# Maxima of a causal segment in whole rows of key blocks: fewer weight loads, diagonals copied from every bank

## The chip, the cores and the metric

The kernel runs on one core of a Trainium2 chip. The metric is the device time of one execution in microseconds; the median of several runs counts. TensorE is called PE (its weight loads PEld), VectorE DVE, ScalarE ACT, GpSimd POOL, and the queue that issues most DMAs SP.

## The reference

Two attention blocks with 32 heads of 16 dimensions read the same 2048 x 512 input, and a sigmoid gate mixes their outputs. Side A is full softmax attention over 2048 keys. Side B works in four segments of 512: causal softmax attention inside a segment, mixed with a linear memory of the earlier segments.

```python
def _B_ref(x, wq, wk, wv, wo, beta):
    ...
    ar = jnp.arange(L)
    mask = (ar[:, None] < ar[None, :]) * (-1e9)
    ...
    for s in range(N):
        qs, ks, vs = q[:, :, s], k[:, :, s], v[:, :, s]
        logits = jnp.einsum("bhqd,bhkd->bhqk", qs, ks) * scale + mask
        p = _softmax(logits, axis=-1)
        a_dot = jnp.einsum("bhqk,bhkd->bhqd", p, vs)
        ...
        o = g * a_mem + (1.0 - g) * a_dot
        ...

g = _sigmoid((x * gate_w).sum(-1, keepdims=True))
out = g * _A_ref(x, A_wqkv, A_wo) + (1 - g) * _B_ref(x, B_wq, B_wk, B_wv, B_wo, B_beta)
```

## The kernel before

The program has two parts. The first, about 330 us long, projects the input into queries, keys and values for both sides. The second, the main loop, does attention. Its work is cut into units: an A unit is four heads against one chunk of 512 queries and all 2048 keys; a B unit is four heads in one segment of 512 queries and keys. There are 32 of each, and in the main loop an A and a B unit alternate.

The order of all instructions is written out by hand in slots. An A unit has 64 slots, a B unit 10, so a pair has 74. A slot n has a score product into one of three PSUM banks `st` (line 652: 50 rows, 128 keys against 512 queries), an exponential on ACT (line 675, 672 for two of B's ten) and, 96 slots ahead for a later unit, one *part of maxima*: `max_part` (line 207) fills one of four PSUM banks `sm` by products (line 204), and the row maxima are taken from it. Maxima have to be known before the scores, because their negatives enter the score product as two extra rows. After every third slot comes a burst of value products (line 708) or of output products (line 785). Score products and products for maxima use different halves of the array's rows in turn, because heads 0, 1 lie in partitions 0 to 63 and heads 2, 3 in partitions 64 to 127; `r` says which half.

An A part is one product of 128 queries by 512 keys and one reduction by DVE (line 219) to one column. A B unit has ten parts, five for each half `r`, placed at every seventh slot of the 74, at slots 6, 13, 20, ... 69 (at every third slot for the first and for the last two units). In a segment of four blocks of 128, query block s needs key blocks 0 to s, the last of them under the causal mask. Before the change the five parts (i = 0 to 4) of a half are:

- i = 0, 1: four products of 128 columns, each a diagonal block of its own (query blocks 0 and 2, or 1 and 3, of two heads). ACT copies the bank to an SBUF tile `dg` (line 230), POOL masks it (`affine_select`, line 231), and eight slots later (`MASK_T`) DVE reduces the tile (line 234).
- i = 2, 3: query block 1 against key block 0 (128 columns) and query block 3 against key blocks 0 to 2 (384 columns), reduced by DVE from PSUM (line 240).
- i = 4: query block 2 against key blocks 0 and 1 for two heads (2 x 256 columns), reduced by DVE from PSUM (line 244).

So a bank was read either by ACT or by DVE. The tiles `dg` rotate through three buffers. The partial maxima lie in a tile `pmB`; nine slots after the unit's last part `finish_max` reduces them (line 182; line 180 for A), POOL rounds them, and eight slots and a little later PE transposes them (line 194). DVE's other work in the main loop is small: reciprocals and factors for the normalisation (lines 759 to 763).

Of the kernel before, what the change touches and what calls it, by code (L numbers as in the profile page):

```python
# [10 lines left out]
F32 = mybir.dt.float32  # L11
F32R = mybir.dt.float32r
AF = mybir.ActivationFunctionType
ALU = mybir.AluOpType
AX = mybir.AxisListType
# [7 lines left out]
CH = 512  # L23
# [24 lines left out]
def gated_mix(ctx, tc, x, xT, wqkv, a_wo, b_wq, b_wk, b_wv, b_wo, beta, gate_w, out):  # L48
    nc = tc.nc
# [43 lines left out]
    mp = ctx.enter_context(tc.tile_pool(name="mp", bufs=2))  # L93
# [18 lines left out]
    for k in range(NU):  # L112
        mine = {u: iter(range(32)) for u in range(2)}
        bs = [k - 1] if 0 < k < NU - 1 else [k - 1, k] if k else []
        start, apart = (34, 3) if k == 1 else (6, 7) if k < NU - 1 else (24, 3)
        theirs = {r: [(unit("B", b), (r, i)) for b in bs for i in range(5)] for r in range(2)}
        for p in range(64 + 10 * len(bs)):
            r = (len(maxs) + 1) % 2
            i = (p - start) // apart
# [42 lines left out]
    def rows(t, h, n):  # L162

        return t[64 * (h // 2):64 * (h // 2) + n, h % 2]
# [4 lines left out]
    late = []  # L169


    pmB = [mp.tile([128, 2, 4, 8], F32, name=f"pmB{i}", bufs=1) for i in range(2)]
    for t in pmB:
        nc.gpsimd.memset(t, -3.0e38)

    def finish_max(u):
        nm = mp.tile([128, 4, 4], F32, tag="nm", name="nm")
        pm = pmt.pop(u)
        if u[0] == "A":
            nc.vector.tensor_reduce(nm, pm, axis=AX.X, op=ALU.max, negate=True)  # L180
        else:
            nc.vector.tensor_reduce(nm.rearrange("p h (a b) -> p (h a) b", b=2),
                                    pm.rearrange("p b h (a k) -> p (h a) b k", a=2), axis=AX.X, op=ALU.max, negate=True)

        ms = mp.tile([128, 2, 2, 2, 4], F32R, tag="ms", name="ms")
        nv = nm.rearrange("p (r h) s -> p r h s", r=2)
        nc.gpsimd.tensor_copy(ms[:, :, 0], nv)  # L187
        nc.gpsimd.tensor_sub(ms[:, :, 1], nv, ms[:, :, 0].bitcast(F32))
        return ms
# [10 lines left out]
    def blocked(ps):  # L200
        return ps.rearrange("p (b t) -> p b t", t=128)

    def max_product(ps, u, h, s, n0, n, k, k0=0):
        nc.tensor.matmul(ps[:, n0:n0 + n], rows(qt[u][:, :, s * 128:(s + 1) * 128], h, 48), rows(k[:, :, k0:k0 + n], h, 48),  # L204
                         start=True, stop=True)

    def max_part(m, bank):

        u, (r, i) = maxs[m]
        side, g, c = u  # L210
        if u not in pmt:
            pmt[u] = mp.tile([128, 4, 4, 4], F32, tag="pmA", name="pm") if side == "A" else pmB[(c * NG + g) % 2]
        pm = pmt[u]
        ps = bank()
        if side == "A":

            kc, s, h = i // 8, i % 8 // 2, 2 * r + i % 2
            max_product(ps, u, h, s, 0, CH, kt_[u, kc])
            nc.vector.tensor_reduce(pm[:, h, s, kc:kc + 1], ps, axis=AX.X, op=ALU.max)  # L219
        else:  # L220


            k = kt_[u, c]
            h0 = 2 * r
            if i < 2:
                for n in range(4):
                    b = i + 2 * (n % 2)
                    max_product(ps, u, h0 + n // 2, b, 128 * n, 128, k, 128 * b)
                dg = dp.tile([128, 4, 128], F32, tag="dg", name="dg")
                nc.scalar.copy(dg, blocked(ps))  # L230
                nc.gpsimd.affine_select(out=dg, in_=dg, pattern=[[0, 4], [-1, 128]], base=0, channel_multiplier=1,  # L231
                                        compare_op=ALU.is_ge, fill=MASKED)
                to = pm[:, i, h0:h0 + 2, 3::4] if i == 0 else pm[:, i, h0:h0 + 2, 1::6]
                todo.append((m + MASK_T, lambda: nc.vector.tensor_reduce(  # L234
                    to, dg.rearrange("p (h s) t -> p h s t", h=2), axis=AX.X, op=ALU.max)))
            elif i < 4:
                h = h0 + i - 2
                max_product(ps, u, h, 1, 0, 128, k)
                max_product(ps, u, h, 3, 128, 384, k)
                nc.vector.tensor_reduce(pm[:, 1, h, 3:7], blocked(ps), axis=AX.X, op=ALU.max)  # L240
            else:
                for f in range(2):
                    max_product(ps, u, h0 + f, 2, 256 * f, 256, k)
                nc.vector.tensor_reduce(pm[:, 0, h0:h0 + 2, 4:6], ps.rearrange("p (h b t) -> p h b t", h=2, b=2), axis=AX.X,
                                        op=ALU.max)
        if m == last_max[u]:
            def finish():
                late.append((m + MASK_T + 2 + LATE_T, u, finish_max(u)))
            todo.append((m + (MASK_T + 1 if side == "B" else 0), finish))
# [28 lines left out]
    with ExitStack() as p0:  # L278
# [5 lines left out]
        wk1 = p0.enter_context(tc.tile_pool(name="wk1", bufs=1))  # L284
# [162 lines left out]
        def betas():  # L447

            ps = me_ps.tile([128, CH], F32, tag="me", name="bt")
            spread = wk1.tile([8, 2, 128], F32, name="spread")  # L450
            one8 = identf[0:8, 0:8]
            nc.vector.tensor_copy(spread[:, 0].rearrange("p (d h) -> p d h", h=8), one8.unsqueeze(1).broadcast_to([8, DH, 8]))
            nc.vector.tensor_copy(spread[:, 1].rearrange("p (h q) -> p h q", q=16), one8.unsqueeze(2).broadcast_to([8, 8, 16]))
            for i, to in enumerate((gh, ogh)):
                nc.tensor.matmul(ps[:, NO * i:NO * i + NO], spread[:, i], beta8, start=True, stop=True)
                nc.scalar.activation(to, ps[:, NO * i:NO * i + NO], AF.Sigmoid)
            nc.vector.tensor_scalar(ogh, ogh, -1.0, 1.0, op0=ALU.mult, op1=ALU.add)
        post_at(20, 2, betas)

        def gate_logit(xg, b, col):  # L460
# [82 lines left out]
        def some_max():  # L543
            m = mnext[0]
            if m == LEAD:
                return
            loads(m + 3 + PRE)
            for i in range(4):
                max_part(m + i, lambda: me_sm.tile([128, CH], F32, tag="sm", name="sm"))
            run_todo(m + 3)  # L550
            mnext[0] += 4
            run_late(me_ps, "me", mnext[0])
# [46 lines left out]
    dp = ctx.enter_context(tc.tile_pool(name="dp", bufs=3, reuse_waits="tile"))  # L599
# [257 lines left out]
    n = 0  # L857
    while n < nS or queue or beside or filled[0] < len(fill):
        for f in beside.pop(n, []):
            f()  # L860
        if n < nS:
            score_part(n)
        m = n + LEAD
        if m < nS:
            loads(m + PRE)

            def bank():
                i = free.pop(0)
                free.append(i)
                return banks[i]  # L870
            max_part(m, bank)
        run_todo(m)
        if n % BURST == BURST - 1 or n >= nS:
            if shared:
                for _ in range(4):
                    shared.pop(0)()
            else:
                some_values(n, MOST + jam(n) if n < nS else 8)

            if any(e[0] < m + 1 for e in late):  # L880
                run_late(st_ps, "st", m + 1)
            else:
                if filled[0] < len(fill) and fill[filled[0]][0] <= n:
                    fill[filled[0]][1]()
                    filled[0] += 1
        n += 1
    octet("A", NO - 1, last, None, vector=True)
    assert len(stored) == len(units)
    for b in range(4):
# [3 lines left out]
        t = fr.tile([128, D], F32, tag="vM" if b % 2 else "res", name="res", bufs=2)  # L893
# [4 lines left out]
def build():  # L898
    import concourse.bacc as bacc
    nc = bacc.Bacc("TRN2", target_bir_lowering=False, num_devices=1)  # L900
    shapes = {"x": (S, D), "xT": (D, S), "wqkv": (D, 3 * D), "a_wo": (D, D), "b_wq": (D, D), "b_wk": (D, D),
              "b_wv": (D, D), "b_wo": (D, D), "beta": (H,), "gate_w": (D,)}
    args = [nc.dram_tensor(n, s, F32, kind="ExternalInput").ap() for n, s in shapes.items()]
    out = nc.dram_tensor("out", (S, D), F32, kind="ExternalOutput").ap()
    with tile.TileContext(nc) as tc:
        gated_mix(tc, *args, out)
    return nc
# [23 lines left out]
```

## Time and profile before

| what | value |
|---|---|
| median of 3 runs (lowest to highest) | 1891.73 us (1890.13 to 1895.54) |
| the profiled execution | 1898.7 us, its span 1896.7 us |
| busy share of the span: PE, PEld, DVE, ACT, POOL | 99%, 53%, 84%, 80%, 17% |
| products for maxima of B units (line 204) | 896, of them 640 with 128, 128 with 256 and 128 with 384 columns |
| mean of one reduction of 512 elements (lines 219, 240, 234) | 685, 685, 679 ns |
| mean of one copy of 128 x 512 to `dg` (line 230) | 596 ns |

Durations of single instructions overlap with those of the next on the same engine, so the distance of two starts says what one costs in a row. A line of a timeline gives start and length in us, engine, line, operation, tiles, shapes and count; in square brackets stand idle time and what ended it.

### The profile page before, as it was taken

The numbers are of one execution on the slowest core, as the hardware profiler recorded it, in microseconds if no ns is written. First come the engines' busy times: TensorE is split into PE (matmuls) and PEld (weight loads), VectorE is DVE, ScalarE is ACT, GpSimd is POOL, SyncE is SP. The second block draws the span as 40 slices with busy tenths as digits, with TensorE's granted clock in tenths as the row PEclk, the third lists the DMA queues.
The fourth block names the chain that finished last, engine by engine and source line by source line (L and its number), as shares of the span: only waits on it lengthen the run. The fifth ranks groups of instructions, "written<-read, shape, count | busy, mean of one in ns | idle before, by whom it ended". The sixth has DMA issues, their size and how long they took to land.

```text
span 1896.7 us, 46501 instructions
## 1 busy us (share of the span) xinstructions
PE 1873.7 (99%) x18137; PEld 1013.2 (53%) x18137; DVE 1596.6 (84%) x2746; ACT 1508.4 (80%) x2929; POOL 315.0 (17%) x514
## 2 busy tenths in 40 slices
PE   9999999999999999999999999999999999999998
PEld 7887776455555554444444444444444454554555
DVE  4234777799999999999999999999999999999810
ACT  5445444798888898888888888888888888888883
POOL 3001222011111111111112111212111211111210
PEclk9999999799999999999999999999999999999999
DMA  7567655234233434344434343434343334343221
GB/s 241 194 226 248 200 192 179 80 109 131 87 110 86 110 86 120 96 107 106 107 101 112 101 112 101 112 101 113 101 109 104 108 98 114 101 113 101 76 60 41
DMA packets 124170, 227.31 MB, mean 120 GB/s; under 512 B 34952, under 2 KB 49960, under 8 KB 123440
## 3 DMA queue, kind: packets, MB, share of 16 engines
q1 hardware_dynamic: 122592, 223.24, 41.3%
q8 instruction: 144, 2.36, 0.5%
q0 software_dynamic: 1072, 0.58, 0.1%
q14 instruction: 74, 0.61, 0.1%
q10 hardware_dynamic: 288, 0.52, 0.1%
HBM read 155.52 MB, written 67.52 MB: 118 GB/s over the span
## 4 chain that ended last, share of the span: by engine, by line
PE 92%; ACT 2%; DMA 2%; DVE 1%; issue 1%; POOL 1%; SPq 0%; ACTq 0%; POOLq 0%; DVEq 0%
PE ops L708 31%; PE st L652 28%; PE sm L204 14%; PE pr L315 11%; PE ops L785 6%; ACT p L675 1%; PE sm L785 1%; POOL mn L375 1%; PE mt_ps L194 1%; PE num L497 1%; ACT dg L230 0%; DMA raw<-xT 0%; DMA qdB<-q 0%; DMA raw<-wqkv 0%; PE mps L528 0%
## 5 line engine op out<-in xcount | busy, mean ns | idle before, releaser
L675 ACT ACTIVATE p<-st 128x512 f32<-128x512 f32 x2304 | 1221.8, 604 | 183.3 <-PE sm L204 145.8
L219 DVE TENSOR_REDUCE pm<-sm 128x1 f32<-128x512 f32 x2048 | 1283.2, 685 | 72.1 <-PE sm L204 59.0
L204 PE MATMUL sm<-kA,qA 48*128 48x512 f32 x2048 | 742.1, 446 | 0.4 <-DVE pm L219 0.4
L652 PE MATMUL st<-qA,kA 50*128 50x512 f32 x2048 | 697.1, 439 | 3.9 <-ACT p L675 3.5
L708 PE MATMUL ops<-p,vA 128*17 128x512 f32 (+3 forms) x5848 | 561.0, 473 | 0.7 <-DMA vA<-vdA 0.7
L652 PEld LDWEIGHTS st<-qA,kA 50*128 50x128 f32 x2048 | 334.9, 186 | 422.0 <-ACT p L675 354.9
L204 PEld LDWEIGHTS sm<-kA,qA 48*128 48x128 f32 x2048 | 334.0, 185 | 20.8 <-DVE pm L219 7.1
L708 PEld LDWEIGHTS ops<-p,vA 128*17 128x17 f32 x5848 | 110.3, 96 | 176.9 <-issue 154.5
L204 PE MATMUL sm<-kB,qB 48*128 48x128 f32 (+2 forms) x896 | 170.9, 294 | 0.0
L204 PEld LDWEIGHTS sm<-kB,qB 48*128 48x128 f32 x896 | 137.2, 189 | 9.1 <-DVE pm L219 2.3
L231 POOL TENSOR_SCALAR_AFFINE_SELECT dg<-dg 128x512 f32<-128x512 f32 x128 | 81.4, 636 | 296.8 <-ACT dg L230 296.8
L187 POOL CAST ms<-nm 128x16 fp32r<-128x16 f32 x64 | 12.7, 198 | 651.7 <-DVE nm L180 402.1
L652 PE MATMUL st<-qB,kB 50*128 50x384 f32 (+3 forms) x512 | 119.3, 341 | 0.6 <-ACT mt L196 0.2
L378 DVE TENSOR_TENSOR q<-full,q 128x512 fp32r<-128x512 f32 x64 | 44.1, 690 | 87.5 <-ACT q L371 87.5
L652 PEld LDWEIGHTS st<-qB,kB 50*128 50x128 f32 x512 | 71.4, 185 | 65.8 <-ACT p L675 52.3
L656 POOL TENSOR_SCALAR_AFFINE_SELECT p<-p 128x512 f32<-128x512 f32 x128 | 78.9, 637 | 91.5 <-ACT p L675 89.3
L240 DVE TENSOR_REDUCE pmB<-sm 128x4 f32<-128x512 f32 x128 | 87.7, 685 | 0.5 <-PE sm L204 0.5
L234 DVE TENSOR_REDUCE pmB<-dg 128x4 f32<-128x512 f32 x128 | 86.9, 679 | 0.0
L708 PE MATMUL ops<-p,vB 128*17 128x128 f32 (+3 forms) x1192 | 86.5, 398 | 0.1
L370 ACT COPY full<-pr 128x512 f32<-128x512 f32 x64 | 37.4, 584 | 51.6 <-PE pr L315 51.4
L230 ACT COPY dg<-sm 128x512 f32<-128x512 f32 x128 | 76.3, 596 | 1.1 <-DVE pmB L234 1.1
L759 DVE RECIPROCAL rec<-rec 128x32 f32<-128x32 f32 x44 | 15.2, 346 | 68.8 <-DMA rec<-odA 36.7
(143 smaller groups left out, 1614.6 us busy)
## 6 DMA issues: line engine op xcount, KB each, us to landing
kA<-kdA SPq DMA_DIRECT2D x256, 128.0 KB
vA<-vdA SPq DMA_DIRECT2D x32, 544.0 KB
kA<-kdA SPq DMA_DIRECT2D x256, 64.0 KB
qdA<-q SPq DMA_DIRECT2D x32, 256.0 KB
kdA<-q SPq DMA_DIRECT2D x32, 256.0 KB
qdB<-q SPq DMA_DIRECT2D x32, 256.0 KB
qA<-qdA SPq DMA_DIRECT2D x64, 128.0 KB
kdB<-q SPq DMA_DIRECT2D x32, 256.0 KB
```

The lines of the kernel that those rows point to most:

```text
L204: nc.tensor.matmul(ps[:, n0:n0 + n], rows(qt[u][:, :, s * 128:(s + 1) * 128], h, 48), rows(k[:, :, k0:k0 + n], h, 48), start=True, stop=True)
L219: nc.vector.tensor_reduce(pm[:, h, s, kc:kc + 1], ps, axis=AX.X, op=ALU.max)
L230: nc.scalar.copy(dg, blocked(ps))
L231: nc.gpsimd.affine_select(out=dg, in_=dg, pattern=[[0, 4], [-1, 128]], base=0, channel_multiplier=1, compare_op=ALU.is_ge, fill=MASKED)
L234: todo.append((m + MASK_T, lambda: nc.vector.tensor_reduce(to, dg.rearrange("p (h s) t -> p h s t", h=2), axis=AX.X, op=ALU.max)))
L240: nc.vector.tensor_reduce(pm[:, 1, h, 3:7], blocked(ps), axis=AX.X, op=ALU.max)
L315: nc.tensor.matmul(ps, l(a, k), r(b, k), start=(n == 0), stop=(n == 11))
L652: nc.tensor.matmul(ps[:, n0:n0 + CH - q0], rows(k[:, :, b * 128:(b + 1) * 128], h, 50), rows(q[:, :, q0:], h, 50), start=True, stop=True)
L656: nc.gpsimd.affine_select(out=x, in_=x, pattern=[[0, 4], [1, 128]], base=0, channel_multiplier=-1, compare_op=ALU.is_ge, fill=0.0)
L675: nc.scalar.activation(p[:, h], ps, AF.Exp, scale=SCALE)
L708: nc.tensor.matmul(ops[32 * h:32 * h + 17, q0:q0 + 128 * w], v[:, 17 * h:17 * h + 17], p[:, h, c0:c0 + 128 * w], start=(i == 0), stop=done ...
L785: nc.tensor.matmul(ps[32 * t:32 * t + 32, 128 * (j % (ps.shape[1] // 128)):128 * (j % (ps.shape[1] // 128)) + 128], held[side, c][:, o, 12 ...
```

## The change

A B unit's ten banks are filled otherwise, with the same number of columns. The five parts of a half are now:

- i = 0, 2 (one head each): query block 0 against key block 0 (128 columns), and query block 2 against key blocks 0 to 2 (384 columns). The bank's first and last blocks are diagonal.
- i = 1: query block 1 against key blocks 0 and 1 for two heads (2 x 256 columns). Its second and fourth blocks are diagonal.
- i = 3, 4 (one head each): query block 3 against key blocks 0 to 3 (512 columns). Its last block is diagonal.

That makes 16 products (and weight loads) a unit in place of 28. From every bank ACT copies the diagonal blocks into a part of a tile `dg` (two blocks for i = 0, 1, 2, one for i = 3, 4), and DVE reduces the other blocks to one or two columns. Two tiles a half are filled that way, one by i = 0 and 1, one by i = 2, 3 and 4; POOL masks a tile after its last copy, and DVE reduces it eight slots after that. In the changed file the product is line 207, ACT's copy line 246, DVE's reduction of a bank line 247, POOL's select line 249 and the reduction of the tile line 255. A small tile of the first part shares another tile's memory to make room for the longer `pmB`.

```diff
-    pmB = [mp.tile([128, 2, 4, 8], F32, name=f"pmB{i}", bufs=1) for i in range(2)]
+    pmB = [mp.tile([128, 96], F32, name=f"pmB{i}", bufs=1) for i in range(2)]
...
-            if i < 2:
-                for n in range(4):
-                    b = i + 2 * (n % 2)
-                    max_product(ps, u, h0 + n // 2, b, 128 * n, 128, k, 128 * b)
-                dg = dp.tile([128, 4, 128], F32, tag="dg", name="dg")
-                nc.scalar.copy(dg, blocked(ps))
+            h = h0 + (0, 0, 1, 0, 1)[i]
+            kind = (0, 1, 0, 2, 2)[i]
+            col = pm[:, 0:64].rearrange("p (b h k) -> p b h k", b=2, h=4)
+            if kind == 0:
+                max_product(ps, u, h, 0, 0, 128, k)
+                max_product(ps, u, h, 2, 128, 384, k)
+                diag, rest, to = blocked(ps)[:, 0::3], ps[:, 128:384], col[:, 0, h, 4:5]
+            elif kind == 1:
+                for f in range(2):
+                    max_product(ps, u, h0 + f, 1, 256 * f, 256, k)
+                diag, rest, to = blocked(ps)[:, 1::2], blocked(ps)[:, 0::2], col[:, 1, h0:h0 + 2, 1:2]
+            else:
+                max_product(ps, u, h, 3, 0, CH, k)
+                diag, rest, to = blocked(ps)[:, 3:4], ps[:, 0:384], col[:, 1, h, 4:5]
+            if i in (0, 2):
+                dgs[r] = dp.tile([128, 4, 128], F32, tag="dg", name="dg")
+            dg = dgs[r]
+            d0 = (0, 2, 0, 2, 3)[i]
+            nc.scalar.copy(dg[:, d0:d0 + diag.shape[1]], diag)
+            nc.vector.tensor_reduce(to, rest, axis=AX.X, op=ALU.max)
+            if i in (1, 4):
                 nc.gpsimd.affine_select(out=dg, in_=dg, pattern=[[0, 4], [-1, 128]], base=0, channel_multiplier=1,
                                         compare_op=ALU.is_ge, fill=MASKED)
-                to = pm[:, i, h0:h0 + 2, 3::4] if i == 0 else pm[:, i, h0:h0 + 2, 1::6]
+                at0, apart = (8 * h0, 34) if i == 1 else (8 * h0 + 8, 31)
+                cols = pm[:, at0:at0 + 2 * apart].rearrange("p (g s) -> p g s", s=apart)[:, :, 0:7:6]
                 todo.append((m + MASK_T, lambda: nc.vector.tensor_reduce(
-                    to, dg.rearrange("p (h s) t -> p h s t", h=2), axis=AX.X, op=ALU.max)))
-            elif i < 4:
-                h = h0 + i - 2
-                max_product(ps, u, h, 1, 0, 128, k)
-                max_product(ps, u, h, 3, 128, 384, k)
-                nc.vector.tensor_reduce(pm[:, 1, h, 3:7], blocked(ps), axis=AX.X, op=ALU.max)
-            else:
-                for f in range(2):
-                    max_product(ps, u, h0 + f, 2, 256 * f, 256, k)
-                nc.vector.tensor_reduce(pm[:, 0, h0:h0 + 2, 4:6], ps.rearrange("p (h b t) -> p h b t", h=2, b=2), axis=AX.X,
-                                        op=ALU.max)
+                    cols, dg.rearrange("p (g f) t -> p g f t", g=2), axis=AX.X, op=ALU.max)))
```

More of the change, by code (lines that the diff above doesn't have):

```diff
@@ L169, in gated_mix @@
     late = []
-    pmB = [mp.tile([128, 2, 4, 8], F32, name=f"pmB{i}", bufs=1) for i in range(2)]
+    pmB = [mp.tile([128, 96], F32, name=f"pmB{i}", bufs=1) for i in range(2)]
     for t in pmB:
         nc.gpsimd.memset(t, -3.0e38)
+    dgs = {}
     def finish_max(u):
@@ L182, in finish_max @@
             nc.vector.tensor_reduce(nm.rearrange("p h (a b) -> p (h a) b", b=2),
-                                    pm.rearrange("p b h (a k) -> p (h a) b k", a=2), axis=AX.X, op=ALU.max, negate=True)
+                                    pm[:, 0:64].rearrange("p (b h a k) -> p (h a) b k", b=2, h=4, a=2), axis=AX.X, op=ALU.max,
+                                    negate=True)
         ms = mp.tile([128, 2, 2, 2, 4], F32R, tag="ms", name="ms")
@@ L449, in betas @@
             ps = me_ps.tile([128, CH], F32, tag="me", name="bt")
-            spread = wk1.tile([8, 2, 128], F32, name="spread")
+            spread = wk1.tile([128, CH], F32, tag="mn", name="spread")[0:8].rearrange("p (i m) -> p i m", m=128)
             one8 = identf[0:8, 0:8]
```

## The prediction, made blind

> **What bounds the kernel now.** I read the page first, then busy time by stage, then the timelines of single engines through one segment unit.
>
> ```profile
> span 1896.7 us, 46501 instructions
> PE 1873.7 (99%) x18137; PEld 1013.2 (53%) x18137; DVE 1596.6 (84%) x2746; ACT 1508.4 (80%) x2929; POOL 315.0 (17%) x514
> PE 92%; ACT 2%; DMA 2%; DVE 1%; issue 1%; POOL 1%; SPq 0%; ACTq 0%; POOLq 0%; DVEq 0%
> 370.00:740.00 370.00, 369.34 (x3681) 185.90 (x3679) 360.81 (x617) 328.96 (x649) 55.06 (x101) 1.00 0.38 106
> 740.00:1508.00 768.00, 763.29 (x7671) 357.28 (x7669) 740.46 (x1268) 675.83 (x1332) 132.03 (x223) 1.00 0.40 105
> 1508.00:1760.00 252.00, 250.63 (x3100) 130.07 (x3104) 239.13 (x407) 218.13 (x431) 43.46 (x73) 1.00 0.37 100
> ```
>
> The last three rows give a stretch, its length, then busy time of PE, PEld, DVE, ACT and POOL. PE looks like the bound (99% busy, 92% of the chain), though its ends are modelled. But VectorE (DVE) is busy 97.5% of the first stretch, 96.4% of the second and 94.9% of the third: what it gains in work or waiting has little room.
>
> PE works in bursts: three score products (st), three products for maxima (sm), then value products. A burst runs from one first st to the next.
>
> ```profile
> 1108.06 0.49 PE L652 MATMUL st<-qA,kA 50*128 50x512 f32 x1
> ...
> 1108.46 0.39 PE L204 MATMUL sm<-kB,qB 48*128 48x384 f32 x1
> ...
> 1110.00 0.50 PE L652 MATMUL st<-qA,kA 50*128 50x512 f32 x1
> ...
> 1111.87 0.50 PE L652 MATMUL st<-qA,kA 50*128 50x512 f32 x1
> ...
> 1112.45 0.40 PE L204 MATMUL sm<-kB,qB 48*128 48x256 f32 x2
> ...
> 1113.76 0.49 PE L652 MATMUL st<-qA,kA 50*128 50x512 f32 x1
> ...
> 1115.65 0.50 PE L652 MATMUL st<-qA,kA 50*128 50x512 f32 x1
> ...
> 1117.52 0.50 PE L652 MATMUL st<-qA,kA 50*128 50x512 f32 x1
> ...
> 1119.42 0.50 PE L652 MATMUL st<-qA,kA 50*128 50x512 f32 x1
> ...
> 1123.17 0.50 PE L652 MATMUL st<-qA,kA 50*128 50x512 f32 x1
> ...
> 1123.75 0.58 PE L204 MATMUL sm<-kB,qB 48*128 48x128 f32 x4
> ...
> 1125.24 0.50 PE L652 MATMUL st<-qA,kA 50*128 50x512 f32 x1
> ```
>
> With A banks alone a burst takes 1.89 us (from 1113.76); with a bank of two 256-wide products also 1.89 (from 1111.87); with 128+384 it takes 1.94 (from 1108.06), with four 128-wide ones 2.07 (from 1123.17). Narrow products cost PE 0.05 and 0.18 a bank.
>
> **TensorE's part.** Per segment unit, four banks of 4x128 and four of 128+384 become four of 128+384 and four of one 512; the two of 2x256 stay. That is 4 x 0.13 + 4 x 0.05 = 0.72 us a unit, 23 us over 32 units where PE sets the pace, 0 where DVE does.
>
> ```profile
> L204 PEld LDWEIGHTS sm<-kB,qB 48*128 48x128 f32 x896 | 137.2, 189 | 9.1 <-DVE pm L219 2.3
> ```
>
> A load's row of 0.19 us is the ceiling: 12 loads fewer would be 2.3 us a unit. The bursts, not this row, decide, since most of a load lies under other products. The Trainium skill ("TensorE: Matmul & The Clock Gate", LDWEIGHTS) counts columns over 1.2 per load, 107 ns here, so 1.28 us a unit if all lay open; by that the 24 units of the later stretches would be 0.56 us better each, and the forecast 13 us lower, 1890. The bursts bear out a little over half of it.
>
> **VectorE's work.** Before, a unit has ten reductions of 512 elements: six of banks, four of diagonal tiles. After, it has six of 256 and four of 384 straight from the banks, and still four of diagonal tiles.
>
> ```profile
> 1076.74 0.21 DVE L182 TENSOR_REDUCE nm<-pmB 128x16 f32<-128x64 f32 x1
> ...
> 1082.19 0.68 DVE L234 TENSOR_REDUCE pmB<-dg 128x4 f32<-128x512 f32 x1
> 1083.15 1.89 DVE L219 TENSOR_REDUCE pm<-sm 128x1 f32<-128x512 f32 x3 [0.28 <-PE sm L204]
> ...
> 1087.07 0.69 DVE L219 TENSOR_REDUCE pm<-sm 128x1 f32<-128x512 f32 x1 [0.55 <-PE sm L204]
> 1087.67 0.68 DVE L234 TENSOR_REDUCE pmB<-dg 128x4 f32<-128x512 f32 x1
> ...
> 1113.65 0.68 DVE L244 TENSOR_REDUCE pmB<-sm 128x4 f32<-128x512 f32 x1
> 1114.33 1.29 DVE L219 TENSOR_REDUCE pm<-sm 128x1 f32<-128x512 f32 x2
> 1115.53 0.34 DVE L759 RECIPROCAL rec<-rec 128x32 f32<-128x32 f32 x1
> ...
> 1116.08 2.48 DVE L219 TENSOR_REDUCE pm<-sm 128x1 f32<-128x512 f32 x4
> 1118.47 0.68 DVE L244 TENSOR_REDUCE pmB<-sm 128x4 f32<-128x512 f32 x1
> 1119.07 2.48 DVE L219 TENSOR_REDUCE pm<-sm 128x1 f32<-128x512 f32 x4
> 1121.58 0.22 DVE L180 TENSOR_REDUCE nm<-pm 128x16 f32<-128x64 f32 x1
> 1121.72 3.07 DVE L219 TENSOR_REDUCE pm<-sm 128x1 f32<-128x512 f32 x5
> 1124.70 0.21 DVE L182 TENSOR_REDUCE nm<-pmB 128x16 f32<-128x64 f32 x1
> ```
>
> Starts count here, since rows overlap: 512 elements take 0.597 us (1121.72 to 1124.70 in five), 64 take 0.14 (1121.58 to 1121.72), so 256 take 0.34 and 384 take 0.47 in between. A unit's work is 10 x 0.597 = 5.97 before and 6 x 0.34 + 4 x 0.47 + 4 x 0.597 = 6.3 after: +0.3 us, 10 us over 32 units, out of 1.7 us of idle per 48 us (the period: 1076.74 to 1124.70).
>
> **The new wait.** A bank's PSUM is now read by two engines, and the built program orders them: each reduction of a B bank waits for ScalarE's copy of its diagonal, where it waited for PE alone. That copy stands in ACT's queue behind the burst's exponentials; behind the waiting reduction stand the next A banks' reductions, and behind those PE's next use of the banks. No bank of the old kernel is read by both engines, so I price it by the nearest rows.
>
> ```profile
> 1112.41 1.58 ACT L675 ACTIVATE p<-st 128x512 f32<-128x512 f32 x3 [0.30 <-PE sm L204]
> L230 ACT COPY dg<-sm 128x512 f32<-128x512 f32 x128 | 76.3, 596 | 1.1 <-DVE pmB L234 1.1
> L809 ACT COPY res<-ops 128x256 f32<-128x256 f32 x23 | 8.6, 374 | 0.2 <-PE ops L785 0.2
> ```
>
> The bank multiplied at 1112.45 is reduced at 1113.65. Its burst's third exponential ends at 1113.99; a 128-wide copy behind it (256 elements fewer save 0.22, so 128 take about 0.26) lands at about 1114.1, or up to 0.13 later without overlap. DVE would wait about 0.45 us there. It is 0 where DVE is late anyway and 0.6 at most; I take 0.3 to 0.45 wherever DVE is caught up. On ACT itself six copies of 0.37 and four of 0.26 replace four of 0.60: +0.9 us a unit by rows, less by overlap, under the 0.30 us that ACT idles in each burst. POOL's four selects and all DMAs stay as they are. Without that cover they would cost 0.9 us a unit, 29 in all. The three rotating diagonal tiles still suffice: a unit opens its four at slots 6, 13, 34 and 41, and the first is reduced at 28, before the fourth reuses its buffer.
>
> The Trainium skill ("PSUM — Partial Sum Buffer", PSUM bank collisions raise a hardware error) has it that two engines must not touch one bank and quadrant at once, reads against reads included. That is the rule that speaks against this change; the built program agrees in that it waits, no run shown here has the case.
>
> **Where the late reductions move.** Diagonal tiles are reduced eight slots after their last copy. Before, the four stood at slots 14, 21, 28 and 35 of the unit's 74; after, at 28, 35, 70 and 77. The first two now lie beside VectorE's idle time: 0.28 behind 1082.19, 0.55 ahead of 1087.67. Slots 70 and 77 are about 1119.6 and 1124.6, where bursts take 1.89 and DVE needs 3 x 0.597 = 1.79 of it, so it makes up 0.10 a burst. What DVE can be late by is seen at 1115.53: reciprocal and factor push 0.55 us in (to 1116.08), and the next bursts still take 1.87 and 1.90. So four banks absorb about 0.55 us; what lies above stalls PE.
>
> Followed from 1113.65 with the change: the wait less the shorter reduction leaves 0.45 - 0.13 = 0.3; two bursts on, the factors make it 0.3 - 0.2 + 0.55 = 0.65, 0.1 over. At slot 70, two bursts later, 0.55 - 0.2 - 0.13 + 0.6 is 0.8, 0.25 to 0.3 over; at slot 77, with the small reduction at 1121.58 in between, 0.55 - 0.2 + 0.14 + 0.6 is 1.1, 0.55 over. Sum 0.9; with 0.2 for the waits at slots 34 to 55 it is 1.1 us a unit, between 0.3 (the waits cost nothing, one late reduction finds room) and 2.
>
> **The sum.** Second stretch, 16 units: -0.72 + 1.1 = +0.4 each, +6.4. First stretch, 8 units, DVE nearly always busy: PE's saving counts little, the +0.3 of work and 0.2 of waits count: +0.5 each, +4. The remaining 8 units, with more room on DVE: +0.2 each, +1.6. Together +12 us. The profiled execution took 1898.7 us (2.0 around its span), 7 above the median of 1891.73; it would become 1910.7, and the median 1903.7. Some 0.3%, 5.7 us, is what a measurement can tell.
>
> **Rivals.**
> - *Forecast, slower by some 12 us* (0.55), 1897 to 1915.
> - *Faster*: PE is the bound and the four banks absorb about 1.1 us, not 0.55, or the copies land before DVE arrives. Then 24 units keep 0.72 (-17), 8 pay 0.3 (+2): 1877 us. For it: PE's 92% of the chain. Against: 96.4% DVE, and waits that the rows put at 0.45. It decides as soon as stalls per unit stay under 0.5. With loads more in the open than the bursts say, it would be faster still. 0.23.
> - *No change*: stalls of 0.5 to 0.9 a unit eat the saving, 1886 to 1897. 0.15.
> - *Waits that nothing hides*: ten of 0.35 and 0.3 of work, less 1.7 of idle, is 2 us a unit, 64 us: 1956. It needs DVE caught up before every B bank though it is the bound; both at once hardly hold. 0.07.
>
> That the change doesn't do what it says is out: the built program has 16 products a unit in place of 28.
>
> The range takes in the forecast, no change and most of the faster case: 1876 to 1920. Faster by over 0.3%: 0.23. Within: 0.15. Slower: 0.55 + 0.07 = 0.62.
>
> **What would show it.** In the profile after: bursts with B banks at 1.89 and 1.94, none at 2.07 (PE's saving); reductions of B banks idle until an ACT copy, some ten a unit (the new wait); PE idle ahead of sm products for DVE around slots 70 to 78 (the moved reductions); DVE's share of the second stretch up while the stretch is longer. If DVE shows no idle for ACT copies, or bursts after slot 70 stay at 1.89, the forecast is wrong and the kernel is faster.

## The result and the profile after

| | before | after |
|---|---|---|
| median of 4 runs (lowest to highest) | 1892.43 us (1890.13 to 1895.54) | 1924.33 us (1922.31 to 1929.76) |
| the profiled execution, its span | 1898.7 us, 1896.7 us | 1924.95 us, 1923.2 us |

The changed kernel is slower by 31.9 us: ratio 1.0163, interval 1.0146 to 1.018. The direction was forecast, the size was not: 1903.7 was given, with 1920 as the upper end.

First the lines of the page of the kernel after that answer to those shown of before (span, engines, chain), then the same three stretches (busy time of PE, PEld, DVE, ACT, POOL).

```profile
span 1923.2 us, 45986 instructions
PE 1904.0 (99%) x17753; PEld 1002.0 (52%) x17753; DVE 1603.4 (83%) x2874; ACT 1521.0 (79%) x3121; POOL 314.7 (16%) x514
PE 88%; DVE 4%; ACT 4%; DMA 3%; issue 1%; POOL 1%; SPq 0%; ACTq 0%; POOLq 0%; DVEq 0%
```

```profile
370.00:740.00 370.00, 368.25 (x3545) 177.68 (x3541) 356.79 (x637) 326.98 (x685) 54.12 (x98) 1.00 0.37 102
740.00:1508.00 768.00, 764.97 (x7299) 348.32 (x7301) 723.07 (x1296) 664.07 (x1391) 130.44 (x221) 1.00 0.39 102
1508.00:1760.00 252.00, 251.11 (x2921) 126.97 (x2917) 234.03 (x419) 215.31 (x451) 43.04 (x71) 1.00 0.37 101
```

PE has 384 fewer products and loads, and is shown busy longer (1904.0 us against 1873.7). The same number of products is busy for 1860.6 us in `e1_copy_from_sbuf` below, so some of the waiting is counted in this row, and it can't tell work from waiting. VectorE's share of the second stretch fell from 96.4% to 94.1% (723.07 of 768). It has more to do and does it at a slower pace, so it waits. The groups of instructions say for what (busy us, mean ns, then idle time ahead of them and what ended it); first the one row of before:

```profile
L219 DVE TENSOR_REDUCE pm<-sm 128x1 f32<-128x512 f32 x2048 | 1283.2, 685 | 72.1 <-PE sm L204 59.0 <-PE st L652 2.8
```

and after:

```profile
L222 DVE TENSOR_REDUCE pm<-sm 128x1 f32<-128x512 f32 x2048 | 1273.8, 681 | 18.0 <-PE sm L207 17.1 <-PE st L663 0.4
L247 DVE TENSOR_REDUCE pmB<-sm 128x1 f32<-128x384 f32 (+2 forms) x320 | 152.2, 476 | 81.1 <-ACT dg L246 77.3
L246 ACT COPY dg<-sm 128x256 f32<-128x256 f32 (+1 forms) x320 | 109.6, 343 | 1.9 <-DVE pmB L255 1.8
```

Before, VectorE idled 72 us ahead of the A banks' reductions, mostly for PE: it had caught up and PE was next. After, it idles 77 us ahead of the B banks' reductions for ScalarE's copy, and only 18 us for PE: it is behind nearly all the time. ScalarE's copies hardly wait (1.9 us). The waits themselves (total us, times, longest) name the second half of the chain; the first row is of before, the next two of after:

```profile
PEld sm L204 <- DVE pm L219: 9.5, 38, 0.7
```

```profile
DVE pmB L247 <- ACT dg L246: 77.3, 172, 0.8
PEld sm L207 <- DVE pm L222: 47.9, 153, 0.7
```

172 of 320 bank reductions wait, 0.45 us each, and PE waits for an A bank 153 times where it was 38. One B bank in the timelines of ACT, DVE and PE (start, length):

```profile
1106.02 0.38 ACT L246 COPY dg<-sm 128x256 f32<-128x256 f32 x1
1106.43 0.42 DVE L247 TENSOR_REDUCE pmB<-sm 128x2 f32<-128x256 f32 x1 [0.60 <-ACT dg L246]
1106.78 0.68 DVE L222 TENSOR_REDUCE pm<-sm 128x1 f32<-128x512 f32 x1
1107.37 0.68 DVE L255 TENSOR_REDUCE pmB<-dg 128x4 f32<-128x512 f32 x1
1107.97 3.07 DVE L222 TENSOR_REDUCE pm<-sm 128x1 f32<-128x512 f32 x5
1110.96 0.41 DVE L247 TENSOR_REDUCE pmB<-sm 128x1 f32<-128x256 f32 x1
```

```profile
1108.95 0.49 PE L663 MATMUL st<-qA,kA 50*128 50x512 f32 x1
1111.33 0.50 PE L663 MATMUL st<-qA,kA 50*128 50x512 f32 x1
1113.24 0.50 PE L663 MATMUL st<-qA,kA 50*128 50x512 f32 x1
```

The copy ends at 1106.40, the reduction starts at 1106.43 after 0.60 us of idle, and from there to 1110.96 VectorE has no gap. PE's burst from 1108.95 takes 2.38 us (to 1111.33); it holds a bank of 128+384. By the records, the second stretch has 57 such bursts, with a median of 2.11 us; before it was 1.94 (64 bursts).

### The profile page after: what moved, and what is told of

It reads as the page before. It is cut to its first block, busy times and chain, and to the rows that moved or that the text cites. A ratio compares the mean times of both kernels' runs of the same rounds, so it can differ in the third digit from the quotient of the medians.

```text
span 1923.2 us, 45986 instructions
## 1 busy us (share of the span) xinstructions
PE 1904.0 (99%) x17753; PEld 1002.0 (52%) x17753; DVE 1603.4 (83%) x2874; ACT 1521.0 (79%) x3121; POOL 314.7 (16%) x514
## 4 chain that ended last, share of the span: by engine, by line
PE 88%; DVE 4%; ACT 4%; DMA 3%; issue 1%; POOL 1%; SPq 0%; ACTq 0%; POOLq 0%; DVEq 0%
PE ops L719 29%; PE st L663 26%; PE sm L207 14%; PE pr L326 10%; PE ops L796 5%; DVE pm L222 2%; ACT p L686 2%; DMA raw<-xT 1%; POOL mn L386 1%; PE num L508 1%; PE sm L796 1%; PE mt_ps L197 0%; DVE pmB L255 0%; DMA vs<-wqkv 0%; DMA qdA<-q 0%
## 5 line engine op out<-in xcount | busy, mean ns | idle before, releaser
L686 ACT ACTIVATE p<-st 128x512 f32<-128x512 f32 x2304 | 1241.9, 606 | 202.2 <-PE sm L207 151.0
L207 PE MATMUL sm<-kA,qA 48*128 48x512 f32 x2048 | 764.5, 453 | 2.4 <-DVE pm L222 2.2
L247 DVE TENSOR_REDUCE pmB<-sm 128x1 f32<-128x384 f32 (+2 forms) x320 | 152.2, 476 | 81.1 <-ACT dg L246 77.3
L207 PE MATMUL sm<-kB,qB 48*128 48x128 f32 (+3 forms) x512 | 153.8, 361 | 0.0
L246 ACT COPY dg<-sm 128x256 f32<-128x256 f32 (+1 forms) x320 | 109.6, 343 | 1.9 <-DVE pmB L255 1.8
L207 PEld LDWEIGHTS sm<-kB,qB 48*128 48x128 f32 x512 | 85.2, 187 | 11.7 <-DVE pm L222 7.4
L796 PE MATMUL ops<-woA,vA 128*32 128x128 f32 x1664 | 66.9, 278 | 0.6 <-ACT oraw L723 0.2
```

Source lines behind the costliest of these rows:

```text
L246: nc.scalar.copy(dg[:, d0:d0 + diag.shape[1]], diag)
L247: nc.vector.tensor_reduce(to, rest, axis=AX.X, op=ALU.max)
L686: nc.scalar.activation(p[:, h], ps, AF.Exp, scale=SCALE)
L796: nc.tensor.matmul(ps[32 * t:32 * t + 32, 128 * (j % (ps.shape[1] // 128)):128 * (j % (ps.shape[1] // 128)) + 128], held[side, c][:, o, 12 ...
```

## The experiments

Ratios are to the kernel before, run beside each group of experiments on the same chip; its medians there were 1893.41 (e1 to e4), 1892.61 (e5 to e8), 1891.81 (e9 to e11) and 1893.47 us (e12). Three theories: W, VectorE's reduction of a bank is ordered behind ScalarE's copy from it; L, the diagonal reductions that moved to slots 70 and 77; S, ScalarE's ten copies hold up the exponentials.

**Taking the order away.** `e1_copy_from_sbuf`, on the changed kernel:

```diff
-            nc.scalar.copy(dg[:, d0:d0 + diag.shape[1]], diag)
+            nc.scalar.copy(dg[:, d0:d0 + diag.shape[1]], identf.unsqueeze(1).broadcast_to([128, diag.shape[1], 128]))
```

> The changed kernel, but ScalarE's 320 copies into the diagonal tiles read an identity matrix in SBUF and not the bank (the diagonal's maxima are left out). ScalarE, GpSimd and the late reductions keep their work; VectorE's reductions of banks wait for TensorE alone. Theory W (the waits of VectorE for ScalarE's copies cost most): the waits go and about 1.2 of some 2 us of stalls per unit with them, 1890 to 1900 us. Theory L (the diagonal reductions that moved to slots 70 and 77 cost most): hardly better, 1916 to 1924. Theory S (ScalarE's ten copies hold up the exponentials): unchanged, 1920 to 1926.

1881.74 us (6 runs), ratio 0.9932 (0.9909 to 0.9954): 42.6 us less than the changed kernel, with all its reductions where they were and all copies on ScalarE. L and S fall, W stands, though it had given 1890 to 1900 us: more came back than was expected.

`e5_reduce_from_sbuf` takes the other reader away:

```diff
-            nc.vector.tensor_reduce(to, rest, axis=AX.X, op=ALU.max)
+            one = identf[:, 0:1]
+            still = one.unsqueeze(1).broadcast_to([128, 2, 128]) if kind == 1 else one.broadcast_to([128, rest.shape[-1]])
+            nc.vector.tensor_reduce(to, still, axis=AX.X, op=ALU.max)
```

> The changed kernel with VectorE's 320 bank reductions reading a constant in SBUF in place of the bank (the maxima of the blocks off the diagonal are left out); ScalarE's copy is then the only reader of each bank. Theory W (the two reads of one bank, one after the other, hold the bank too long, 42.6 us over 320 banks, 0.13 us each): with one reader left the time falls to 1878 to 1888 us, as it did with VectorE as the only reader. Theory S (ScalarE's copies come late, and a bank held by them costs by itself): at least 1900 us.

1880.39 us, ratio 0.9934 (0.9913 to 0.9955), the same. Its waits have no row of VectorE for a copy, and PE's for the exponentials, for ScalarE's copies and for an A bank are

```profile
PEld st L665 <- ACT p L688: 399.3, 831, 0.9
PEld st L665 <- ACT dg L246: 55.4, 91, 0.9
PEld sm L207 <- DVE pm L222: 22.7, 67, 0.7
```

PE waits for the copies as long as in the kernel after (53.7 us there) without harm: either reader alone is cheap, the pair as built is not.

**TensorE alone.** `e2_products_alone`: the kernel before, its readers kept (so that they take their maxima from other blocks), with 16 products a unit:

```diff
-                for n in range(4):
-                    b = i + 2 * (n % 2)
-                    max_product(ps, u, h0 + n // 2, b, 128 * n, 128, k, 128 * b)
+                max_product(ps, u, h0 + i, i, 0, 128, k)
+                max_product(ps, u, h0 + i, i + 2, 128, 384, k)
...
-                max_product(ps, u, h, 1, 0, 128, k)
-                max_product(ps, u, h, 3, 128, 384, k)
+                max_product(ps, u, h, 3, 0, CH, k)
```

> The kernel before with the products of the change alone: four banks of 128+384 in place of 4x128, four of one 512 in place of 128+384 (some maxima are of the wrong blocks); every bank is still read by one engine, and the diagonal reductions stand where they stood. W, L and S alike: TensorE's 0.72 us a unit come through in 24 units, 1874 to 1884 us. If VectorE sets the pace in the later stretches too, TensorE's saving is worth nothing: 1888 to 1893.

1884.78 us (10 runs), ratio 0.9953 (0.9937 to 0.9968): 8.6 us, or 0.27 us a unit, just short of what was expected. From the other side `e12_old_products`, e1 with 28 products in place of 16:

```diff
-                max_product(ps, u, h, 0, 0, 128, k)
-                max_product(ps, u, h, 2, 128, 384, k)
+                for n in range(4):
+                    b = n // 2 * 2
+                    max_product(ps, u, h, b, 128 * n, 128, k, 128 * b)
...
-                max_product(ps, u, h, 3, 0, CH, k)
+                max_product(ps, u, h, 1, 0, 128, k)
+                max_product(ps, u, h, 3, 128, 384, k)
```

> The changed kernel with ScalarE's copies reading a constant in SBUF (one reader of each bank, the diagonal blocks left out) and the 28 products a unit of the kernel before in place of 16: TensorE's part alone, seen from the other side, against the 1881.7 us of the same readers with 16 products. If the weight loads are worth what they were worth with the old readers: 1881.7 + 8.6 = 1890 us (1887 to 1894). If they are worth the 0.72 us a unit that the bursts gave, in 24 to 32 units: 1899 to 1905 us. If the readers' pace hides them: 1880 to 1885 us.

1891.76 us, ratio 0.9998 (0.9981 to 1.0015): 10.0 us above e1, and the same as the kernel before. So the products are worth 9 to 10 us, and the rest of the change without the order (six more copies a unit, the shorter reductions, the late reductions at their new slots) costs nothing that can be measured; the interval is 3 us wide to either side.

The busy time of VectorE in the two fits with 12 loads fewer bringing so little: with 28 products (e12, first row) it is busy 740.20 of the second stretch's 768 us, with 16 (e1) 745.59, 97.1%.

```profile
740.00:1508.00 768.00, 764.43 (x7627) 356.52 (x7627) 740.20 (x1321) 680.34 (x1417) 130.57 (x220) 1.00 0.41 105
740.00:1508.00 768.00, 763.91 (x7482) 339.93 (x7479) 745.59 (x1332) 685.73 (x1429) 133.46 (x224) 1.00 0.41 105
```

**Where the waits lie.** `e3_every_third_slot` puts the B banks at every third slot, so that all late reductions come long before slot 70:

```diff
-        start, apart = (34, 3) if k == 1 else (6, 7) if k < NU - 1 else (24, 3)
+        start, apart = (34, 3) if k == 1 else (6, 3) if k < NU - 1 else (24, 3)
```

> The changed kernel with the ten banks of every middle unit at every third slot from slot 6 to 33, not every seventh to 69: the late diagonal reductions go from slots 70 and 77 to 38 and 41. L: about 0.9 us a unit of stalls goes, 1898 to 1908 us. W: as many waits, now one in each burst, so no better: 1918 to 1935. S: more copies in a row for ScalarE, 1925 to 1940.

1940.19 us, ratio 1.0271 (1.0216 to 1.0326): worse, and above all three ranges. L fails a second time.

```profile
DVE pmB L247 <- ACT dg L246: 78.2, 187, 2.3
```

VectorE waits for the copies about as long in sum as in the changed kernel (77.3 us); why the crowded banks cost 16 us more was not taken apart.

**Turning the order round.** In `e4_reduce_a_slot_later` VectorE doesn't stand and wait, but comes to the bank a slot later:

```diff
-            nc.vector.tensor_reduce(to, rest, axis=AX.X, op=ALU.max)
+            todo.append((m + 1, lambda: nc.vector.tensor_reduce(to, rest, axis=AX.X, op=ALU.max)))
```

> The changed kernel with each B bank's reduction put one slot later in VectorE's order, behind the next A bank's: the copy has 0.6 us more to land. W: VectorE's idle time for copies falls from 77 us to under 25, and the time to 1895 to 1910 us. L and S: within 6 us of 1924.

1921.9 us, ratio 1.0152 (1.012 to 1.0184). VectorE's wait for copies fell from 77.3 to 1.1 us, and almost nothing is won: W had given 1895 to 1910 us, and the time lies where L and S had it. PE now waits for the bank itself:

```profile
PEld sm L207 <- DVE pmB L247: 38.7, 94, 0.9
PE sm L207 <- DVE pmB L247: 8.3, 30, 0.5
```

`e11_late_reduction_alone` is this with e1's copies, thus with one reader of each bank:

> The changed kernel with ScalarE's copies reading a constant in SBUF (the diagonal blocks' maxima are then wrong), and VectorE's reduction of the bank a slot later: one reader of each bank, no wait between the two engines, only a bank that is held about 1 us longer. If what the version with the reduction a slot later lost (1921.9 us) was the late release alone: 1910 to 1925 us. If it needed the second reader: 1880 to 1892 us.

1924.61 us, ratio 1.0173 (1.0145 to 1.0201), with the same wait:

```profile
DVE pm L222 <- PE sm L207: 79.5, 161, 2.6
PEld sm L207 <- DVE pmB L247: 37.6, 93, 0.9
```

So e4 lost its time to the late reduction alone, with or without a second reader, and W is not refuted by it. PE's wait for the bank is one way; but VectorE also waits 79.5 us for the products of A banks, where it was 45.2 in e1, and whether that is a result of PE's wait or a loss of its own these runs don't tell. In `e6_reduce_then_copy` VectorE reads first and ScalarE comes a slot later; in `e9_reduce_then_copy_at_once` right behind:

```diff
-            nc.scalar.copy(dg[:, d0:d0 + diag.shape[1]], diag)
             nc.vector.tensor_reduce(to, rest, axis=AX.X, op=ALU.max)
+
+            def copy():
+                nc.scalar.copy(dg[:, d0:d0 + diag.shape[1]], diag)
+                if i in (1, 4):
+                    nc.gpsimd.affine_select(out=dg, in_=dg, pattern=[[0, 4], [-1, 128]], base=0, channel_multiplier=1,
+                                            compare_op=ALU.is_ge, fill=MASKED)
+            todo.append((m + 1, copy))      # e6;  e9: copy()
             if i in (1, 4):
-                nc.gpsimd.affine_select(out=dg, in_=dg, pattern=[[0, 4], [-1, 128]], base=0, channel_multiplier=1,
-                                        compare_op=ALU.is_ge, fill=MASKED)
...
```

> The changed kernel with the order of the two reads turned round: VectorE reduces the bank first, ScalarE's copy of the diagonal blocks comes a slot later in program order. Theory W, as a matter of how long a bank is held: still two reads in a row, 1905 to 1930 us. If the cost is only that VectorE, at 96% busy in this stretch, is made to wait: 1880 to 1892 us, since ScalarE (79% busy) can wait.

> The changed kernel with the two reads of a bank exchanged and both in one slot: VectorE reduces, ScalarE copies right behind. Theory W (what costs is VectorE waiting behind ScalarE, which comes to the bank later than VectorE would): 1884 to 1900 us, near the 1888 us of the copy a slot later; the bank comes free earlier than there, but ScalarE waits some 0.38 us a bank for VectorE (the reduction ended 1.14 us after the product where nothing delayed it, ScalarE came at 0.76 us). Rival (any engine's wait for the other costs the same, ScalarE's holding up the exponentials): 1905 to 1930 us.

e6: 1888.06 us (10 runs), ratio 0.9968 (0.9955 to 0.9981), 36 us better than the changed kernel and, of the kernels here that keep the whole computation, the only one ahead of the kernel before. e9: 1934.73 us, ratio 1.0226 (1.0196 to 1.0256), the worst but one. Waits of e6:

```profile
PEld st L665 <- ACT p L688: 398.5, 818, 0.9
PEld sm L207 <- DVE pm L222: 19.0, 55, 0.7
ACT dg L249 <- DVE pmB L246: 16.0, 44, 0.9
```

and of e9:

```profile
PEld st L665 <- ACT p L688: 475.7, 961, 1.3
ACT dg L249 <- DVE pmB L246: 68.3, 154, 1.4
PEld sm L207 <- DVE pm L222: 14.1, 41, 0.7
```

In e9 ScalarE, busy only 79% of its span, waits 68 us for VectorE, 0.44 us each, and what is queued behind it, the exponentials, comes late: PE waits 77 us more for them than in e6. My expectation of e9 was wrong; the rival in it was nearer, though the time is 5 us above its range too: a wait is dear in either of the two engines. In e6 neither waits much (16 us in all). VectorE reduces a bank when it gets to it, ScalarE goes on with the next exponential and copies 0.9 us after the reduction started:

```profile
1080.04 0.42 DVE L246 TENSOR_REDUCE pmB<-sm 128x2 f32<-128x256 f32 x1
1080.50 3.68 DVE L222 TENSOR_REDUCE pm<-sm 128x1 f32<-128x512 f32 x6
```

```profile
1080.96 0.37 ACT L249 COPY dg<-sm 128x256 f32<-128x256 f32 x1
```

The next table is worked out from the records' starts and ends between 340 and 1760 us. For the B banks (289 to 298 a kernel) it has the mean us after the end of the bank's last product (an end that is modelled). For the A banks (some 1840 to 1910) it has the same start, and the number of those that were released too late, which means that PE's next load for that bank began less than 60 ns after the release:

| | VectorE starts on a B bank | the bank is released | VectorE starts on an A bank | A banks released too late |
|---|---|---|---|---|
| one reader (e1) | 0.68 | 1.14 | 0.67 | 222 |
| after | 1.16 | 1.63 | 0.98 | 528 |
| VectorE a slot later (e4) | 1.67 | 2.14 | 0.65 | 233 |
| the same, one reader (e11) | 1.66 | 2.13 | 0.65 | 225 |
| ScalarE a slot later (e6) | 0.65 | 1.81 | 0.65 | 182 |
| ScalarE right behind VectorE (e9) | 0.59 | 1.44 | 0.57 | 114 |

The changed kernel puts VectorE 0.48 us later on its own bank and then 0.31 us later on all the others. e4 spares the others and releases its bank at 2.14 us, too late for 174 of 293 B banks' next loads (gap under 60 ns); e6 at 1.81 us, too late for 117 of 297, at a mean gap of 0.25 us against 0.13. How long a bank is held is thus not what made the change slow: e6 holds its banks longer than the changed kernel and is 36 us faster. And in e9 neither VectorE nor the release is late, so that its loss is left to ScalarE's wait.

**The same wait put into the kernel before.** `e8_old_with_small_copies` has a ScalarE copy of 8 columns from each of the six banks that VectorE reads, ahead of its reduction, in both branches:

```diff
+                nc.scalar.copy(few, ps[:, 0:8])
                 nc.vector.tensor_reduce(pm[:, 1, h, 3:7], blocked(ps), axis=AX.X, op=ALU.max)
```

> The kernel before, with one small ScalarE copy (8 columns) added from each of the six banks of a unit that VectorE alone reads, ahead of VectorE's reduction of it; weight loads, products and reductions stay as they were. Theory W: 6 banks x 0.13 us x 32 units = 25 us if the second reader costs what it costs in the changed kernel, less for so short a copy: 1905 to 1920 us. If a second reader costs nothing by itself: below 1897 us.

1921.54 us, ratio 1.0152 (1.0123 to 1.0181), just above the range of W: 28.9 us over 192 banks, 0.15 us each, for a copy of 0.17 us.

```profile
DVE pmB L242 <- ACT few L241: 25.1, 68, 0.7
PEld sm L205 <- DVE pm L220: 23.6, 91, 0.7
```

`e10_old_small_copies_second` has the same copies behind the reduction, a slot later:

```diff
-                nc.scalar.copy(few, ps[:, 0:8])
                 nc.vector.tensor_reduce(pm[:, 1, h, 3:7], blocked(ps), axis=AX.X, op=ALU.max)
+                todo.append((m + 1, lambda: nc.scalar.copy(few, ps[:, 0:8])))
```

> The kernel before with the small ScalarE copies (8 columns) from the six banks again, now a slot behind VectorE's reduction of the bank in place of ahead of it. Theory W: 1892 to 1900 us (the reversed order left 6 us over 320 banks in the changed kernel, so some 4 us over 192). Rival (a second reader costs in either order): 1912 to 1925 us, as with the copies first.

1896.96 us, ratio 1.0025 (1.0003 to 1.0047): 5 us. The weight loads and the moved reductions have no part in this pair, and the place of the copy, ahead of the reduction or a slot behind it, makes 24 us of difference.

**One reader, all on ScalarE.** `e7_one_reader` keeps the 16 products, copies whole banks and reduces from SBUF:

```diff
-            nc.scalar.copy(dg[:, d0:d0 + diag.shape[1]], diag)
-            nc.vector.tensor_reduce(to, rest, axis=AX.X, op=ALU.max)
+            dg = dp.tile([128, 4, 128], F32, tag="dg", name="dg")
+            nc.scalar.copy(dg, blocked(ps))
...
+            todo.append((m + MASK_T, lambda: nc.vector.tensor_reduce(to, src, axis=AX.X, op=ALU.max)))
```

> The sixteen weight loads kept, and each bank read once: ScalarE copies the whole bank to SBUF (ten copies of up to 512 columns in a unit), GpSimd masks the diagonal blocks there, VectorE reduces from SBUF eight slots later. The whole computation is kept. Theory W: 1880 to 1890 us, if ScalarE's longer copies (about 2.9 us more in a unit, an estimate from its copies of 256 and 512 columns) find room in its idle time of 5.7 of 48 us. Theory S: 1900 us or more, with PE waiting for ScalarE's copies.

1928.25 us, ratio 1.0183 (1.0155 to 1.0212). W's range was missed; the time is in that of S.

```profile
PEld st L655 <- ACT p L678: 463.3, 932, 1.3
L243 ACT COPY dg<-sm 128x512 f32<-128x512 f32 x320 | 191.5, 598 | 5.3 <-DVE pmB L248 4.7 <-PE ops L711 0.3 <-DVE nm L186 0.2
```

Copies of 0.60 us in place of 0.34 are 82 us more on ScalarE, and PE waits 64 us more for exponentials than in e5 (399.3). ScalarE idled 5.8 us per 48 us before (768 less 675.83 us over 16 units), more than the copies need, but it seems not where they need it. VectorE's reductions lie elsewhere in this kernel as well; that share was not measured apart.

## Why the prediction missed

Its steps against the runs, in us over the 32 units:

| step | forecast | measured |
|---|---|---|
| TensorE's narrow products | -17 in 24 units, -23 at most | -8.6 (e2), -10.0 (e12 to e1) |
| VectorE's work, and late reductions at slots 70 and 77 | +10, and +0.9 a unit in 24 | -1.7 together (e12 to before, its interval holds 0) |
| VectorE's wait for the copies | +0.2 a unit | +42.6 (after to e1), 1.33 a unit |

The measured column adds to 1892.43 - 10.0 - 1.7 + 42.6 = 1923.3, against 1924.33. It has to, since its steps lead from before over e12 and e1 to after; what bears it out from outside is e2 for the first row and e8 against e10 for the last.

- **The step that failed is the wait's term in the sum.** Its price was right: 0.3 to 0.45 us was taken for one wait, and the 172 waits are 0.45 us on average, the upper end. Their count and what becomes of them were wrong. I let waits be "0 where DVE is late anyway" and kept 0.2 us a unit; 172 in 32 units are 5.4 a unit or 2.4 us, and 1.33 us a unit is what they cost in time. What made VectorE "late anyway" was an average: left alone it starts on a B bank 0.68 us after the product, ScalarE's copy ends at 1.13 us (e1, where the copy waits for nothing). The 72 us that VectorE idled before stood for catching up, not for room; 54 of them went, and the A banks that were released too late went up from 241 before (222 in e1) to 528.
- **The late reductions were a false cost.** The same slots with no ordered reads are as fast as the kernel before; the argument from slots 70 and 77 charged 0.9 us a unit (0.1 of it carried on from the wait), and that hid how small the term for the wait had been made. The crowding itself is there: in the second stretch of e12, 70 of the 105 A banks released too late lie at slots 68 to 83, before it was 19 of 99. But there are nearly as many fewer at the other slots, and on balance nothing is lost that can be measured. The forecast came as near as it did by luck, because the two errors had opposite signs. Whether the late reductions cost something together with the waits is not shown apart; e8 has the price of the wait, 0.15 us a bank, without them.
- **TensorE's saving was sized too large.** The bursts gave 0.72 us a unit; 0.27 to 0.31 came. The single bursts were read rightly: by the records of the second stretch, those with four 128-wide products had a median of 2.09 us, and with 128+384 in their place in e2 1.94. But only 37 of the stretch's 64 such banks lie in bursts of three A score products, for which these times hold. That VectorE, at 97% in e1, sets the pace of the bursts behind a shortened one fits with the rest and is not shown apart: bursts with no B bank are longer by 0.01 us on average in e2 than before, within their scatter. The prediction had counted on such a pace for the first stretch alone. The estimate from the figure of the Trainium skill ("TensorE: Matmul & The Clock Gate", LDWEIGHTS), 1.28 us a unit, is four times what was measured.
- **VectorE's work** is near: 1596.6 to 1603.4 us busy, +6.8 for a forecast of 10.
- **The signs that were named**: reductions idle until a copy are there, 5.4 a unit where some ten were expected. Bursts with one product of 512 have a median of 1.89 us, as was named, but those with 128+384 have 2.11 where 1.94 was named. PE's waits for VectorE are there, but all over the unit: of 263 A banks released too late in the second stretch, 85 lie at slots 68 to 83. VectorE's share of the stretches fell where it was to rise, and that was the clearest mark of a wait in place of work.
- **The rivals**: "waits that nothing hides" (0.07, 1956 us) had the right mechanism and took every bank for a wait; the runs lie between it and the forecast. The rule of the Trainium skill ("PSUM — Partial Sum Buffer", section "PSUM bank collisions raise a hardware error") was seen as what speaks against the change. The runs agree in that the program keeps the two reads in order; no run here shows a collision. The order costs 0.13 us a bank as built and 0.02 as in e6 (1888.06 less 1881.74 over 320 banks), so the order alone doesn't set the price: who goes first and when does.

What stays open is why 2.14 us to a release cost 40 us (e4) and 1.81 us only 6 (e6). The runs have no point between the two, and they also differ in where VectorE's reduction stands in its queue.

## What to carry to other kernels

Before two engines are given one PSUM bank to read, find out when each of them gets to it by itself, and let the one that comes first, or that has no room, read first; put the other's read behind its next own work, so that neither waits, as long as the bank is released in time. Here an engine at 79% could no more wait than one at 96%, because the work queued behind its wait feeds PE. Idle time that an engine shows for PE can be what lets it catch up, as it was here: a wait taken out of it is not free.

## What the runs showed of the hardware

A copy of 8 columns takes 0.17 us and costs the kernel 0.15 us a bank when VectorE's reduction is ordered behind it (e8), about as much as copies of 256 and 128 columns that take 0.34 on average (0.13 a bank, after to e1). In these two kernels the length of the copy hardly counts; its place does, since the same 8 columns a slot behind the reduction cost 0.03 us a bank (e10, 5 us over 192). And 384 fewer matmuls with their weight loads of 0.19 us each, some 72 us laid end to end, moved the time by 9 to 10 us.
